# Banded scores on four quarters of the array, and five PSUM banks for the first batch's products, in a fused attention, channel-mix and gated-attention kernel

## The chip, the cores and the metric

One core of a Trainium2 chip runs the whole program. The metric is device time in microseconds (us), the median of the runs shown; lower is better. PE is TensorE, DVE VectorE, ACT ScalarE, POOL GpSimd; SP issues most of the DMAs. PSUM, where PE writes its products, has eight banks of 128 partitions x 512 fp32 numbers.

## The reference

Three stages follow each other, for 4 batches of 576 positions and 512 features (8 heads of 64).

```python
def _attn_ref(q, k, v):                      # stage 1: banded attention
    scores = scale * np.matmul(q, k.transpose(0, 1, 3, 2))
    mask_plain = (rel >= 0) & (rel < window)                                   # heads 0-3, window 32
    mask_dil = (rel >= 0) & (rel < window * dilation) & (rel % dilation == 0)  # heads 4-7, dilation 4
    scores = np.where(masks[None, :, :, :], scores, -1000000000.0)
    ...                                      # softmax over the keys
    return np.matmul(attn, v).astype(np.float32)

def _moe_ref(x, mu_k, mu_r, w_k, w_v, w_r):  # stage 2: channel mix
    xk = mu_k * x + (1.0 - mu_k) * x_prev
    xr = mu_r * x + (1.0 - mu_r) * x_prev
    k = np.maximum(xk @ w_k, 0.0)
    v = k * k @ w_v
    r = 1.0 / (1.0 + np.exp(-(xr @ w_r)))
    return (r * v).astype(np.float32)
# stage 3 (_moe2_ref): per position two of four experts, each a causal attention with its own
# wq, wk, wv, wo over the 576 positions
```

## The kernel before

**Stage 1.** A batch has four head pairs: pairs 0 and 1 with the plain window, 2 and 3 with the dilated one, whose positions are sorted by remainder first, so that both are a band. A pair's queries are cut into nine tiles of 64, each against 96 keys. `turn_qk` (L271, L276) makes qT and kT, in which one head of the pair has partitions 0 to 63 and the other 64 to 127. `attn_weights` computes the scores (`products`, L304): for each query tile one 64x64 weight load and 96 columns for each head; head 0 uses array rows 0 to 63 and writes output partitions 0 to 63, head 1 the other half of both. Query tiles 0 to 4 lie in one PSUM bank and 5 to 8 in a second, both with the tag `sc`. In fp32 a product is two passes, so a block of one pair is 2 x 9 x 2 = 36 PE rows. Then for each query tile DVE adds the mask, takes the minimum into `st` (L323) and leaves the scores in `pe`; ACT takes the exponential (L328), DVE scales by the reciprocal sum (L338 to L340). `attn_values`: PE transposes three query tiles of weights (`pt`, L368), ACT copies them (L369), PE multiplies by the values (`av`, L379), ACT copies the result into x (L394). For batches 2 and 3 the weights are turned by DVE and a round trip through DRAM instead, without `pt`. Batch 0's scores also accumulate a mask that PE adds from the identity.

For batch 1 the two banks' products are issued one after the other, each ahead of its own softmax part; for batches 2 and 3 both come first (L289 to L310).

**Stage 2.** Per batch and half c of 288 positions: 4 receptance products z (L532), 8 keys products h (L539), 4 value products v (L555). Each is 12 (z, h) or 24 (v) matmuls of 128x288, high and low parts of fp32 (`product`, L517 to L524). ACT reads z (tanh, L537) and h (ReLU, L543); DVE and ACT make the square's high part kh and low part kl from r (L547 to L553); x is overwritten with z times v (L559). The mixed inputs m, xh and xl come from x (L498 to L502 for batch 0, L513 and L514 for the others, where POOL makes xl).

**PSUM.** `ps` (L60) hands out banks by tag: sc 2, pt 2, av 1, mm 3. All products of stage 2 use `mm`. A tag's banks go round; a product waits until the bank's former content has been read.

**What sets the order.** `goal` (L714) and the loop after it set how many steps of attention (batches 1, then 2 and 3) are written between the steps of the channel mix (batches 0 to 3). A scheduler of the framework then orders each engine's instructions by its own estimates of time; within one engine they run in that order. `together_with(b, 2)` (L527) puts the score products of batches 2 and 3 behind the last matmul of `product` written so far. `load_qk` and `load_v` are issued by SP in order; the queries and keys of pair 2 of batch 1 come behind the mark "window". Names in the rows: sc_1_0_5 is the score bank of batch 1, pair 0, from query tile 5; h_0_1_6 the keys product of batch 0, half 1, slice 6; z_1_0_2 and v_0_1_0 likewise; pt_1_0_2 the third transpose of batch 1, pair 0. The number behind is a serial one.

Of the kernel before, what the change touches and what calls it, by code (L numbers as in the profile page):

```python
# [21 lines left out]
def tile_dilated_attention__rwkv_channel_mix__moe_attention(  # L22
# [17 lines left out]
    nc = tc.nc  # L40
# [5 lines left out]
    CH = 288  # L46
    QB = 64
    WK = QB + 32
# [11 lines left out]
    def ps(tag, name):  # L60
        return psum["pool"].tile([128, 512], F32, tag=tag, name=name, bufs=psum[tag])


    ident = cpool.tile([128, 128], F32, name="ident")
# [62 lines left out]
    def win(dil, t):  # L127

        if t == 0:
            return 0, m_first  # L130
        return QB * t - 32, (m_class.get(t, m_next) if dil else m_next)

    early = {}
# [91 lines left out]
    def attn_pair(ap, b, hp, loaded):  # L225

        qT, kT = turn_qk(ap, b, hp, loaded[0])
        yield
        pe = yield from attn_weights(ap, b, hp, qT, kT)
        yield from attn_values(ap, b, hp, loaded[1], pe)  # L230
# [50 lines left out]
    def attn_weights(ap, b, hp, qT, kT):  # L281

        dil = hp >= NP // 2
        nm = f"{b}_{hp}"
        pe = ap.tile([128, NT, WK], F32, tag="pe", name=f"pe_{nm}", bufs=2)
        st = ap.tile([128, 3, NT], F32, tag="st", name=f"st_{nm}", bufs=2)
        scs = {}

        def products(t0, t1):  # L289

            sc = scs[t0] = ps("sc", f"sc_{nm}_{t0}")
            n = t1 - t0
            if b == 0:
                for j in range(2):
                    h = slice(64 * j, 64 * j + 64)
                    nc.tensor.matmul(sc[h, : n * WK], early["ident"][h, h], early[int(dil)][h, t0:t1, :],
                                     start=True, stop=False)
            for t in range(t0, t1):
                k0, mask = win(dil, t)
                c0 = WK * (t - t0)  # L300
                with together_with(b, 2):
                    for j in range(2):
                        h = slice(64 * j, 64 * j + 64)
                        nc.tensor.matmul(sc[h, c0 : c0 + WK], qT[h, QB * t : QB * t + QB], kT[h, k0 : k0 + WK],  # L304
                                         start=(b > 0), stop=(b > 0 or t == t1 - 1))

        if b > 1:
            for t0, t1 in ((0, 5), (5, 9)):
                products(t0, t1)
            yield  # L310
        for t0, t1 in ((0, 5), (5, 9)):
            if b < 2:
                products(t0, t1)
            sc = scs[t0]
            n = t1 - t0
            if b == 0:
                nc.vector.tensor_reduce(out=st[:, 0, t0:t1], in_=sc[:, : n * WK].rearrange("p (t k) -> p t k", k=WK),
                                        axis=AX.X, op=ALU.min)
            for t in range(t0, t1):
                k0, mask = win(dil, t)  # L320
                c0 = WK * (t - t0)
                if b:
                    nc.vector.tensor_tensor_reduce(  # L323
                        out=pe[:, t, :], in0=sc[:, c0 : c0 + WK], in1=mask, scale=-0.125, scalar=BIG,
                        op0=ALU.add, op1=ALU.min, accum_out=st[:, 0, t : t + 1],
                    )
                if b or not t0 == 5:
                    nc.scalar.activation(  # L328
                        pe[:, t, :], pe[:, t, :] if b else sc[:, c0 : c0 + WK], AF.Exp, bias=st[:, 0, t : t + 1], scale=-1.0,
                        accum_out=st[:, 1, t : t + 1],  # L330
                    )
            if b == 0 and t0 == 5:
                pb = pe[:, t0:t1, :]
                nc.vector.tensor_tensor(pb, st[:, 0, t0:t1].unsqueeze(2).to_broadcast([128, n, WK]),
                                        sc[:, : n * WK].rearrange("p (t k) -> p t k", k=WK), op=ALU.subtract)
                nc.scalar.activation(pb, pb, AF.Exp)
                nc.vector.tensor_reduce(out=st[:, 1, t0:t1], in_=pb, axis=AX.X, op=ALU.add)
            nc.vector.tensor_scalar_add(st[:, 1, t0:t1], st[:, 1, t0:t1], 1e-9)  # L338
            nc.vector.reciprocal(st[:, 2, t0:t1], st[:, 1, t0:t1])
            marks["first weights"] = nc.vector.tensor_mul(pe[:, t0:t1, :], pe[:, t0:t1, :],  # L340
                           st[:, 2, t0:t1].unsqueeze(2).to_broadcast([128, n, WK])).ins
            yield
        return pe
# [14 lines left out]
    def attn_values(ap, b, hp, vw, pe=None, pT=None):  # L358

        dil = hp >= NP // 2  # L360
        nm = f"{b}_{hp}"
        av = None
        for i in range(3):
            if pT is None:
                pt = ps("pt", f"pt_{nm}_{i}")
                pts = ap.tile([WK, 384], F32, tag="pts", name=f"pts_{nm}_{i}", bufs=2)
                for a in range(3):
                    nc.tensor.transpose(pt[:WK, 128 * a : 128 * a + 128], pe[:, 3 * i + a, :], ident)  # L368
                nc.scalar.copy(pts, pt[:WK, :384])  # L369
            for a in range(3):  # L370
                t = 3 * i + a
                cuts = [(0, 64)] if t != 4 else [(0, 32), (32, 64)]
                for u0, u1 in cuts:
                    p0 = QB * t + u0
                    if p0 in (0, 288):
                        av = ps("pt" if pT is not None and p0 else "av", f"av_{nm}_{p0}")
                    with together_with(b, 2):
                        for j in range(2):
                            nc.tensor.matmul(  # L379
                                av[64 * j : 64 * j + 64, p0 % 288 : p0 % 288 + u1 - u0],  # L380
                                vw[:, j, t, :],
                                (pts[:, 128 * a + 64 * j + u0 : 128 * a + 64 * j + u1] if pT is None
                                 else pT[:, 2 * j + u0 // 32 : 2 * j + u1 // 32, t, :]),
                                start=True, stop=True,
                            )
                    p1 = QB * t + u1
                    if p1 in (288, 576):
                        hf = p1 // 288 - 1
                        if dil:
                            dst = X[b][:, hp, 1 : S + 1].rearrange("p (i r) -> p r i", r=4)  # L390
                            dst, src = dst[:, 2 * hf : 2 * hf + 2, :], av[:, :288].rearrange("p (r i) -> p r i", r=2)
                        else:
                            dst, src = X[b][:, hp, 1 + 288 * hf : 289 + 288 * hf], av[:, :288]
                        nc.scalar.copy(dst, src)  # L394
            if (hp, i) == (NP - 1, 2):
                complete.add(b)
            yield
# [129 lines left out]
    def together_with(b, first):  # L527


        return tc.issue_after(marks["product"]) if b >= first and "product" in marks else ExitStack()  # L530

    def receptance(dp, b, c, fo, z, xr, wts):  # L532
        p = ps("mm", f"z_{b}_{c}_{fo}")[:, :CH]
        product(p, wts["r"], xr, range(KT), slice(128 * fo, 128 * fo + 128))


        nc.scalar.activation(z[:, fo, :], p, AF.Tanh, scale=0.5)  # L537

    def keys(dp, b, c, fo, kh, kl, xk, wts):  # L539
        p = ps("mm", f"h_{b}_{c}_{fo}")[:, :CH]  # L540
        product(p, wts["k"], xk, range(KT), slice(128 * fo, 128 * fo + 128))
        r = dp.tile([128, CH], F32, tag="r", name=f"r_{b}_{c}_{fo}", bufs=2)
        nc.scalar.activation(r, p, AF.Relu)  # L543
        if b == 0 and 2 <= fo < 6:
            nc.scalar.activation(r, r, AF.Square)
            nc.scalar.activation(kh[:, fo, :], r, AF.Copy, scale=0.5)
            nc.vector.scalar_tensor_tensor(out=kl[:, fo, :], in0=r, scalar=0.5, in1=kh[:, fo, :].bitcast(F32),  # L547
                                           op0=ALU.mult, op1=ALU.subtract)
            return
        nc.vector.scalar_tensor_tensor(out=r, in0=r, scalar=0.5, in1=p if b else r, op0=ALU.mult, op1=ALU.mult)  # L550
        nc.scalar.copy(kh[:, fo, :], r)  # L551
        half = nc.gpsimd if b == 1 and fo % 2 == 0 and fo < FT - 2 else nc.vector
        half.tensor_sub(kl[:, fo, :], r, kh[:, fo, :].bitcast(F32))  # L553
# [82 lines left out]
    with tc.tile_pool(name="apool", bufs=2, side="left") as ap:  # L636
# [80 lines left out]
        stop = per + 6 * NP * 2 + 3  # L717
# [505 lines left out]
```

## Time and profile before

| | before |
|---|---|
| median of 3 runs | 554.2 us (553.92 to 554.38) |
| profiled execution, its own time | 553.32 us |
| its span in the trace | 551.5 us |
| PE busy | 534.1 us, 97% |
| DVE busy | 350.1 us, 63% |
| ACT busy | 337.9 us, 61% |
| POOL busy | 65.0 us, 12% |

The profile comes from one execution, 0.9 us faster than the median. Sums are made against its own time. Batch 1's attention lies from 88 to about 139 us, beside batch 0's keys and values; the attention of batches 2 and 3 follows, beside the channel mix of batches 1 and 2; stage 3 begins at 356 us. An engine's busy share is an average over these; what a change is worth has to be read in the stretch where it acts. In the timeline, neighbouring matmuls overlap by some 0.16 us (the pipeline), so that the distance of starts, not the duration, is a product's cost.

### The profile page before, as it was taken

The page shows a single profiled execution, that of the slowest core. Times are in us where ns is not written, and L with a number is a line of the kernel's source. Part 1 is how long each engine was busy: PE and PEld are TensorE (multiplying, and loading weights), DVE is VectorE, ACT ScalarE, POOL GpSimd, SP SyncE. Part 2 cuts the span into 40 slices and gives each one's busy share as a digit, 9 for nine tenths or more (in the row PEclk, how much of TensorE's full clock was granted, in tenths as well). Part 3 has the DMA queues.
Part 4 walks back from the last instruction along what each step waited for, and adds up shares of the span by engine and source line. Part 5 has one row for each costly group of instructions (what it writes and reads, how often), then busy time and mean ns, then how long its engine had stood idle before and what let it go on. Part 6 is the DMA issues. An engine that isn't in the chain of part 4 may idle for free.

```text
span 551.5 us, 12506 instructions
## 1 busy us (share of the span) xinstructions
PE 534.1 (97%) x4657; PEld 483.9 (88%) x4657; DVE 350.1 (63%) x1153; ACT 337.9 (61%) x959; POOL 65.0 (12%) x99
## 2 busy tenths in 40 slices
PE   8987989999999999999999999999999999999996
PEld 4657978989999999999999999999977988988763
DVE  3788989775766588276360526438686559566752
ACT  3789988575874484564453525237576667656862
POOL 8500000010342031221032203000000000000000
PEclk9997999999999999999999999999999999999999
DMA  9969386857545663130100420054605615324313
GB/s 168 240 184 285 91 214 144 151 108 137 103 113 128 141 140 79 42 97 13 54 1 1 92 63 1 1 130 97 163 5 126 177 31 130 93 75 115 112 39 96
DMA packets 130173, 57.66 MB, mean 105 GB/s; under 512 B 109928, under 2 KB 117184, under 8 KB 130112
## 3 DMA queue, kind: packets, MB, share of 16 engines
q1 hardware_dynamic: 129392, 55.88, 42.8%
q8 instruction: 37, 0.61, 0.5%
q0 software_dynamic: 416, 0.44, 0.4%
q10 hardware_dynamic: 304, 0.53, 0.3%
q14 instruction: 24, 0.20, 0.1%
HBM read 34.42 MB, written 10.03 MB: 81 GB/s over the span
## 4 chain that ended last, share of the span: by engine, by line
PE 85%; ACT 7%; DVE 5%; DMA 2%; issue 1%; SPq 0%; ACTq 0%; DVEq 0%
PE v L524 19%; PE h L524 14%; PE z L524 7%; PE av L1037 5%; PE pv L863 5%; PE po L1123 5%; PE sc L304 4%; PE pt L1000 4%; PE pq L524 4%; PE pk L524 4%; PE av L379 4%; PE sc L949 2%; PE sc L951 2%; PE idle L76 2%; PE pt L368 2%; DMA rqk<-in_q_dram 1%
## 5 line engine op out<-in xcount | busy, mean ns | idle before, releaser
L524 PE MATMUL h<-xh,wk_hi 128*128 128x288 f32 x256 | 76.7, 300 | 1.8 <-ACT r L543 1.7
L524 PE MATMUL h<-xl,wk_hi 128*128 128x288 f32 x256 | 75.7, 296 | 0.6 <-DVE xl L502 0.6
L524 PE MATMUL h<-xh,wk_lo 128*128 128x288 f32 x256 | 75.3, 294 | 0.0
L524 PE MATMUL v<-kh,wv_hi 128*128 128x288 f32 x256 | 74.9, 299 | 0.0
L524 PE MATMUL v<-kh,wv_lo 128*128 128x288 f32 x256 | 74.8, 297 | 0.0
L524 PE MATMUL v<-kl,wv_hi 128*128 128x288 f32 x256 | 74.5, 296 | 0.0
L961 ACT ACTIVATE pe<-pe,st 128x64 f32<-128x64 f32 (+4 forms) x80 | 44.8, 561 | 16.6 <-DVE st L955 16.1
L514 POOL TENSOR_TENSOR xl<-m,xh 128x576 fp32r<-128x576 f32 x24 | 34.7, 1461 | 152.4 <-ACT xh L513 152.4
L524 PEld LDWEIGHTS h<-xh,wk_hi 128*128 128x128 f32 x256 | 47.9, 187 | 3.3 <-ACT r L543 2.7
L524 PEld LDWEIGHTS h<-xl,wk_hi 128*128 128x128 f32 x256 | 48.1, 188 | 0.9 <-DVE xl L502 0.9
L524 PEld LDWEIGHTS v<-kh,wv_lo 128*128 128x128 f32 x256 | 47.8, 188 | 0.6
L524 PEld LDWEIGHTS v<-kh,wv_hi 128*128 128x128 f32 x256 | 47.6, 188 | 0.7 <-DVE r L550 0.2
L524 PEld LDWEIGHTS h<-xh,wk_lo 128*128 128x128 f32 x256 | 48.2, 188 | 0.0
L524 PEld LDWEIGHTS v<-kl,wv_hi 128*128 128x128 f32 x256 | 47.7, 188 | 0.2
L328 ACT ACTIVATE pe<-pe,st 128x96 f32<-128x96 f32 x108 | 39.0, 363 | 13.3 <-DVE st L323 13.3
L543 ACT ACTIVATE r<-h 128x288 f32<-128x288 f32 x64 | 25.6, 406 | 33.6 <-PE h L524 30.1
L955 DVE CUSTOM_DVE_ANT_0 pe<-sc,cmask 128x64 f32<-128x64 f32 (+4 forms) x80 | 33.1, 427 | 17.2 <-PE sc L951 16.7
L499 DVE SCALAR_TENSOR_TENSOR m<-x,mus,m 128x288 f32<-128x288 f32 x64 | 30.6, 517 | 16.3 <-ACT m L498 16.2
L553 DVE TENSOR_TENSOR kl<-r,kh 128x288 fp32r<-128x288 f32 x50 | 30.5, 615 | 15.6 <-ACT kh L551 15.5
L524 PE MATMUL z<-xh,wr_hi 128*128 128x288 f32 x128 | 39.3, 310 | 0.9 <-ACT z L537 0.9
L524 PE MATMUL z<-xl,wr_hi 128*128 128x288 f32 x128 | 38.4, 301 | 0.0
L524 PE MATMUL z<-xh,wr_lo 128*128 128x288 f32 x128 | 38.3, 300 | 0.0
(195 smaller groups left out, 1404.2 us busy)
## 6 DMA issues: line engine op xcount, KB each, us to landing
kk<-kh SPq DMA_DIRECT2D x32, 144.0 KB, 2.8
kl<-kl SPq DMA_DIRECT2D x32, 144.0 KB, 2.8
raw_in_moe_w_k_dram<-in_moe_w_k_dram SPq DMA_DIRECT2D x4, 1024.0 KB, 8.2
raw_in_moe_w_v_dram<-in_moe_w_v_dram SPq DMA_DIRECT2D x4, 1024.0 KB, 6.0
out_dram<-ob SPq DMA_DIRECT2D x14, 256.0 KB, 2.8
rqk<-in_q_dram SPq DMA_DIRECT2D x48, 72.0 KB, 2.5
rqk<-in_k_dram SPq DMA_DIRECT2D x48, 72.0 KB, 2.4
moved<-turned SPq DMA_DIRECT2D x8, 432.0 KB, 3.0
```

The costliest lines, as they stand in the source:

```text
L304: nc.tensor.matmul(sc[h, c0 : c0 + WK], qT[h, QB * t : QB * t + QB], kT[h, k0 : k0 + WK], start=(b > 0), stop=(b > 0 or t == t1 - 1))
L328: nc.scalar.activation(pe[:, t, :], pe[:, t, :] if b else sc[:, c0 : c0 + WK], AF.Exp, bias=st[:, 0, t : t + 1], scale=-1.0, accum_out=st[ ...
L499: nc.vector.scalar_tensor_tensor(out=m, in0=x, scalar=mus[:, 0, w, f : f + 1], in1=m, op0=ALU.mult, op1=ALU.add)
L514: nc.gpsimd.tensor_sub(lo[:, f], m[:, f], hi[:, f].bitcast(F32))
L524: marks["product"] = nc.tensor.matmul(o, w[:, kt, wsl], x[:, kt, :], start=(n == 0), stop=(n == last)).ins
L543: nc.scalar.activation(r, p, AF.Relu)
L553: half.tensor_sub(kl[:, fo, :], r, kh[:, fo, :].bitcast(F32))
L863: nc.tensor.matmul(p, x[:, kt, t0 : t0 + tn], w[:, kt, 512:772], start=(n == 0), stop=(n == 3 * KT - 1))
L955: nc.vector.tensor_tensor_reduce(out=pe[:tn, PO[t] + c0 : PO[t] + c1], in0=sc, in1=m, scale=-0.125, scalar=(BIG if i == 0 else st[:tn, 1, ...
L961: nc.scalar.activation(pb, pb, AF.Exp, bias=st[:tn, 0, t : t + 1], scale=-1.0, accum_out=st[:tn, 2, t : t + 1])
L1037: ins = nc.tensor.matmul(av1[p0 : p0 + 64, q0 - 64 : q1 - 64], vh[kb][:kn], w[:kn, c0 : c0 + q1 - q0], start=(kb == blocks[0]), stop=(kb = ...
L1123: nc.tensor.matmul(sums[t], x[:, t0 : t0 + 128], w[:, h, :], start=(h == 0 and n == 0), stop=(h == 1 and n == 2))
```

## The change

Two edits.

First, for batches 1 to 3 all 18 score products of a pair are issued together (`all_products`), in the order of query tiles 5, 0, 6, 1, 7, 2, 8, 3, 4. Query tiles 5 to 8 write the other half of the output partitions: head 0 in partitions 64 to 127, head 1 in 0 to 63. Rows 0 to 63 or 64 to 127 of the array with output half 0 or 1 make four 64x64 quarters. `attn_values` reads the heads of these query tiles from the swapped half. Batch 1 thus has both banks of scores before its first softmax; batch 0 is as before.

Second, `bank` gives batch 0's receptance and keys products banks by turns from mm, pt, mm, pt, mm: five banks for what had three. The 23rd of these products is h_0_1_6, and it gets `pt`.

```diff
@@ attn_weights
-            if b == 0:
-                for j in range(2):
-                    ...
+            for j in range(2):
+                h = slice(64 * j, 64 * j + 64)
+                nc.tensor.matmul(sc[h, : n * WK], early["ident"][h, h], early[int(dil)][h, t0:t1, :],
+                                 start=True, stop=False)
             for t in range(t0, t1):
                 k0, mask = win(dil, t)
                 c0 = WK * (t - t0)
-                with together_with(b, 2):
-                    for j in range(2):
-                        h = slice(64 * j, 64 * j + 64)
-                        nc.tensor.matmul(sc[h, c0 : c0 + WK], qT[h, QB * t : QB * t + QB], kT[h, k0 : k0 + WK],
-                                         start=(b > 0), stop=(b > 0 or t == t1 - 1))
+                for j in range(2):
+                    h = slice(64 * j, 64 * j + 64)
+                    nc.tensor.matmul(sc[h, c0 : c0 + WK], qT[h, QB * t : QB * t + QB], kT[h, k0 : k0 + WK],
+                                     start=False, stop=(t == t1 - 1))
+
+        def all_products():
+            for t0 in (0, 5):
+                scs[t0] = ps("sc", f"sc_{nm}_{t0}")
+            with together_with(b, 2):
+                for t in (5, 0, 6, 1, 7, 2, 8, 3, 4):
+                    k0 = win(dil, t)[0]
+                    c0 = WK * (t % 5)
                     for j in range(2):
                         h = slice(64 * j, 64 * j + 64)
+                        o = h if t < 5 else slice(64 - 64 * j, 128 - 64 * j)
+                        nc.tensor.matmul(scs[t // 5 * 5][o, c0 : c0 + WK], qT[h, QB * t : QB * t + QB], kT[h, k0 : k0 + WK],
+                                         start=True, stop=True)
+
+        if b >= 1:
+            all_products()
         if b > 1:
-            for t0, t1 in ((0, 5), (5, 9)):
-                products(t0, t1)
             yield
         for t0, t1 in ((0, 5), (5, 9)):
-            if b < 2:
+            if b < 1:
                 products(t0, t1)
@@ attn_values
+                            r = 1 - j if b and t > 4 else j
                             nc.tensor.matmul(
                                 av[64 * j : 64 * j + 64, p0 % 288 : p0 % 288 + u1 - u0],
                                 vw[:, j, t, :],
-                                (pts[:, 128 * a + 64 * j + u0 : 128 * a + 64 * j + u1] if pT is None
-                                 else pT[:, 2 * j + u0 // 32 : 2 * j + u1 // 32, t, :]),
+                                (pts[:, 128 * a + 64 * r + u0 : 128 * a + 64 * r + u1] if pT is None
+                                 else pT[:, 2 * r + u0 // 32 : 2 * r + u1 // 32, t, :]),
@@ receptance, keys
+    used = []
+
+    def bank(b):
+        if b:
+            return "mm"
+        used.append(b)
+        return ("mm", "pt", "mm", "pt", "mm")[len(used) % 5]
-        p = ps("mm", f"z_{b}_{c}_{fo}")[:, :CH]
+        p = ps(bank(b), f"z_{b}_{c}_{fo}")[:, :CH]
-        p = ps("mm", f"h_{b}_{c}_{fo}")[:, :CH]
+        p = ps(bank(b), f"h_{b}_{c}_{fo}")[:, :CH]
```

The code's lines move down: L304 before is L318 after, L524 is L539, L368 L382, L379 L394, L550 L575, L553 L578, L323 L337.

On PE, batch 2's pair 1 among batch 1's receptance products, before:

```order
L524 MATMUL z_1_0_1_2089<-xh_1_0_4_1873,wr_lo_252 128x288
L304 MATMUL sc_2_1_0_2105<-kT_2_1_2064,qT_2_1_2062 64x96 x10
L304 MATMUL sc_2_1_5_2116<-kT_2_1_2064,qT_2_1_2062 64x96 x8
L524 MATMUL z_1_0_2_2125<-xh_1_0_4_1873,wr_hi_251 128x288
L524 MATMUL z_1_0_2_2125<-xl_1_0_4_1874,wr_hi_251 128x288
```

And the end of the same block after the change:

```order
L318 MATMUL sc_2_1_5_2106<-kT_2_1_2064,qT_2_1_2062 64x96 x2
L318 MATMUL sc_2_1_0_2105<-kT_2_1_2064,qT_2_1_2062 64x96 x2
L318 MATMUL sc_2_1_5_2106<-kT_2_1_2064,qT_2_1_2062 64x96 x2
L318 MATMUL sc_2_1_0_2105<-kT_2_1_2064,qT_2_1_2062 64x96 x4
L539 MATMUL z_1_0_2_2125<-xl_1_0_4_1874,wr_hi_251 128x288
```

The two banks take turns by pairs of heads instead of coming one behind the other; the block stands one matmul further down among the same products.

On PE, batch 1's pair 0 and the keys product h_0_1_6, before:

```order
L524 MATMUL h_0_1_5_1362<-xh_0_1_3_995,wk_lo_272 128x288
L304 MATMUL sc_1_0_0_1287<-kT_1_0_1283,qT_1_0_1281 64x96 x10
L304 MATMUL sc_1_0_5_1329<-kT_1_0_1283,qT_1_0_1281 64x96 x8
L524 MATMUL h_0_1_6_1409<-xh_0_1_3_995,wk_hi_271 128x288
L524 MATMUL h_0_1_6_1409<-xl_0_1_3_996,wk_hi_271 128x288
```

After the change h_0_1_6 stands behind pair 0's transposes and first values:

```order
L394 MATMUL av_1_0_0_1355<-pts_1_0_0_1350,vw_1_1274 64x64 x6
L394 MATMUL av_1_0_0_1355<-pts_1_0_1_1381,vw_1_1274 64x64 x2
L394 MATMUL av_1_0_0_1355<-pts_1_0_1_1381,vw_1_1274 64x32 x2
L382 MATMUL pt_1_0_2_1396<-ident_66,pe_1_0_1285 96x128 x3
L539 MATMUL h_0_1_6_1409<-xh_0_1_3_995,wk_hi_271 128x288
L539 MATMUL h_0_1_6_1409<-xl_0_1_3_996,wk_hi_271 128x288
L539 MATMUL h_0_1_6_1409<-xh_0_1_3_995,wk_lo_272 128x288
```

Pair 0's scores now stand behind h_0_1_7 and, in front of its transposes, PE has 21 value products, pair 1's scores and 19 more value products. Of the values v_0_1_0, those that read slices 6 and 7 come after h_0_1_6.

On DVE, between pair 1's softmax and pair 2's of batch 1, before:

```order
L550 SCALAR_TENSOR_TENSOR r_0_1_7_1481<-r_0_1_7_1481 128x288
L339 RECIPROCAL st_1_1_1443<-st_1_1_1443 128x4
L340 TENSOR_TENSOR pe_1_1_1442<-pe_1_1_1442,st_1_1_1443 128x384
L553 TENSOR_TENSOR kl_0_1_1016<-r_0_1_6_1422,kh_0_1_1015 128x288
L553 TENSOR_TENSOR kl_0_1_1016<-r_0_1_7_1481,kh_0_1_1015 128x288
L271 STREAM_TRANSPOSE qT_1_2_1585<-rqk_1257 128x144x4
L271 STREAM_TRANSPOSE kT_1_2_1587<-rqk_1257 128x144x4
L271 STREAM_TRANSPOSE qT_1_3_1729<-rqk_1257 128x144x4
```

After:

```order
L271 STREAM_TRANSPOSE kT_1_2_1587<-rqk_1257 128x144x4
L271 STREAM_TRANSPOSE qT_1_3_1729<-rqk_1257 128x144x4
L584 SCALAR_TENSOR_TENSOR x0_212<-z_0_0_847,v_0_0_1_1703 128x288
L575 SCALAR_TENSOR_TENSOR r_0_1_6_1422<-r_0_1_6_1422 128x288
L575 SCALAR_TENSOR_TENSOR r_0_1_7_1490<-r_0_1_7_1490 128x288
L578 TENSOR_TENSOR kl_0_1_1016<-r_0_1_6_1422,kh_0_1_1015 128x288
L578 TENSOR_TENSOR kl_0_1_1016<-r_0_1_7_1490,kh_0_1_1015 128x288
L337 ISA pe_1_2_1589,st_1_2_1590<-sc_1_2_5_1592,m_next_104 128x96
```

The squares and low parts of slices 6 and 7 moved from before pair 2's turning of queries and keys to behind it, directly before pair 2's softmax, which begins with query tile 5 or later. On POOL the second low half xl of batch 1's first half now stands behind the clearing of the new rows of x.

## Rows read from the trace of the kernel before

**Rows 1.** The page: the span, and busy time of each engine.
```profile
span 551.5 us, 12506 instructions
PE 534.1 (97%) x4657; PEld 483.9 (88%) x4657; DVE 350.1 (63%) x1153; ACT 337.9 (61%) x959; POOL 65.0 (12%) x99
```

**Rows 2.** Stretches: bounds, length, busy per engine (count), granted clock, DMA share, GB/s.
```profile
45.72:49.97 4.25, 4.25 (x19) 4.25 (x18) 3.58 (x7) 3.26 (x7) 0.00 (x0) 0.50 1.13 316
62.00:88.14 26.14, 23.75 (x171) 22.41 (x169) 23.86 (x38) 22.01 (x45) 0.10 (x1) 1.00 0.79 206
88.14:139.41 51.27, 50.90 (x595) 46.50 (x595) 37.02 (x156) 33.96 (x131) 2.80 (x3) 1.00 0.68 126
139.41:356.00 216.59, 216.59 (x2012) 212.57 (x2012) 121.98 (x348) 115.03 (x336) 43.59 (x37) 1.00 0.28 66
```

**Rows 3.** PE's waits from 45 to 93: total us, times, longest.
```profile
PE h L524 <- ACT r L543: 1.7, 3, 1.2
PE z L524 <- ACT z L537: 0.9, 2, 0.6
PE h L524 <- DVE xl L502: 0.6, 1, 0.6
```

**Rows 4.** The chain of waits from 50 to 93: start, us, what.
```profile
69.26 1.10 DVE xl L502 x3
...
81.63 5.81 DMA rqk<-in_q_dram
```

**Rows 5.** The chain of waits from 155 to 172.
```profile
155.52 3.20 PE h L524 x24
158.72 1.63 PE sc L304 x36
...
163.75 1.31 PE av L379 x40
```

**Rows 6.** Timeline of PE, 98 to 99.3: start, us, what.
```profile
98.52 0.82 PE L368 MATMUL pt<-ident,pe 128*96 128x128 f32 x6
99.18 0.40 PE L524 MATMUL v<-kh,wv_hi 128*128 128x288 f32 x1
```

**Rows 7.** Instructions of L304 from 142 to 260: ns min/median/max, first and last.
```profile
L304 PE MATMUL sc<-kT,qT x252: 242/243/294, 142.5 to 255.4; 64*64 64x96 f32 x126
```

**Rows 8.** Timeline of PE, 88 to 139: scores and transposes of batches 1 and 2.
```profile
88.14 1.70 PE L304 MATMUL sc<-kT,qT 64*64 64x96 f32 x36
...
93.60 1.70 PE L304 MATMUL sc<-kT,qT 64*64 64x96 f32 x36 [0.37 <-DVE kT L276]
...
116.70 0.75 PE L368 MATMUL pt<-ident,pe 128*96 128x128 f32 x5
117.38 1.04 PE L304 MATMUL sc<-kT,qT 64*64 64x96 f32 x20
...
118.60 0.54 PE L304 MATMUL sc<-kT,qT 64*64 64x96 f32 x6
...
123.70 1.04 PE L304 MATMUL sc<-kT,qT 64*64 64x96 f32 x18
```

**Rows 9.** Timeline of DVE, 88 to 117: start, us, what, idle before and its releaser.
```profile
92.68 0.78 DVE L276 STREAM_TRANSPOSE kT<-rqk 128x576 f32<-128x576 f32 x1
...
96.29 0.46 DVE L553 TENSOR_TENSOR kl<-r,kh 128x288 fp32r<-128x288 f32 x1
...
97.02 0.66 DVE L340 TENSOR_TENSOR pe<-pe,st 128x480 f32<-128x480 f32 x1
...
105.99 1.19 DVE L271 STREAM_TRANSPOSE kT<-rqk 128x576 f32<-128x576 f32 x1 [0.69 <-DMA rqk<-in_k_dram]
...
111.66 0.26 DVE L323 CUSTOM_DVE_ANT_0 pe<-sc,m_next 128x96 f32<-128x96 f32 x1 [1.29 <-PE sc L304]
```

**Rows 10.** Timeline of POOL, 135 to 140.
```profile
138.02 1.43 POOL L514 TENSOR_TENSOR xl<-m,xh 128x576 fp32r<-128x576 f32 x1 [19.96 <-ACT xh L513]
139.38 0.19 POOL L124 MEMSET x<- 128x4 f32 x2
```

More of the change, by code (lines that the diff above doesn't have):

```diff
@@ L292, in products @@
             n = t1 - t0
-            if b == 0:
-                for j in range(2):
-                    h = slice(64 * j, 64 * j + 64)
-                    nc.tensor.matmul(sc[h, : n * WK], early["ident"][h, h], early[int(dil)][h, t0:t1, :],
-                                     start=True, stop=False)
+            for j in range(2):
+                h = slice(64 * j, 64 * j + 64)
+                nc.tensor.matmul(sc[h, : n * WK], early["ident"][h, h], early[int(dil)][h, t0:t1, :],
+                                 start=True, stop=False)
             for t in range(t0, t1):
```

## The prediction

> **What bounds the kernel now.** I read the page's first part, then the busy time in stretches. TensorE (PE) works 97% of the span, DVE, the next, 63% [rows 1]. The stretches show where this is strict: from 139.41 to 356 us, where the attention of batches 2 and 3 stands among the channel mix, PE is busy the whole time, 216.59 us; from 88.14 to 139.41 (batch 1's attention) 50.90 of 51.27; only from 62 to 88.14 does it lose 2.4 us [rows 2]. So a microsecond of PE taken out of the long stretch is a microsecond of time, and nothing else there is. The last stretch (from 356) isn't touched. PE's waits between 45 and 93 us name what the second part of the change works on: 1.7 us of keys products behind ACT's ReLU (three times) and 0.9 us of receptance products behind ACT's tanh, both because a product needs a PSUM bank that the reader has not given back, and 0.6 us behind DVE's low half xl [rows 3]. The chain of waits over the same time doesn't run through PE's banks but through that DVE subtraction and the loads of queries [rows 4]: there PE isn't the only bound.
>
> **Part 1: the scores on four array tiles.** A block (both heads, nine query tiles) is 18 products, each two passes: 36 rows. In the middle of the kernel it takes 1.63 us between keys products of 133 ns [rows 5]; the blocks of pair 0 and 1 of batch 1 read 1.70 with the last product's tail [rows 8]. The full array passes 128 columns of fp32 at about 110 ns: the six transposes' passes go from 98.52 to 99.18, 0.66/6 [rows 6]. For 96 columns that is 110 x 96/128 = 82 ns, an estimate. Two heads side by side then take 9 x 2 x 82 ns = 1.48 us, and with 0.15 of change-over 1.63, what the row says: the two tiles already run at once. With four, query tiles 0 to 4 (two of the array's quarters) and 5 to 8 (the two others) overlap; the fuller quarters hold 5 products: 5 x 2 x 82 = 0.82, plus 0.15 = 0.97. **A block saves 0.66 us.** No row shows four quarters at work. Bounds: nothing is saved, if quarters that share input rows take turns; or the rows come at the pace of the densest small products in the trace, the 40 rows of values in 1.31 us [rows 5], less 0.15, 29 ns each: 36 x 29 ns + 0.15 = 1.19, a saving of 0.44. I take 0.66: the two heads' rows start together now, so issue doesn't hold back a pair.
>
> The Trainium skill ("TensorEngine Tiling (Array Packing)", Tiling Modes) lists four independent 64x64 tiles; but its Gotcha 1: PSUM Pressure says that different row tiles cannot access the same PSUM bank simultaneously. By that the two heads of before, which write one bank, would take 36 x 82 ns + 0.15 = 3.1 us, an estimate; the trace's 1.63 disagrees [rows 5], so I don't let this rule count against the change, which keeps the two heads of one query tile in one bank.
>
> Blocks of batches 2 and 3: eight. Seven, 252 rows, lie after 142 us [rows 7], where PE is all [rows 2]. **Term A: 7 x 0.66 = 4.6 us** (0 to 4.6; 3.1 at the values' pace). On PE the order there hardly moves: the same products stand before and behind the block. DVE gets the upper tiles first, which it reads as fast; after 139 us each block has dozens of products between itself and its values.
>
> **Part 2, and batch 1, from 62 to 139.** Here the order changes, so I count PE's work and its new idle time. Batch 1's four blocks and batch 2's first (PE's scores at 123.70 [rows 8]) save 5 x 0.66 = 3.3. The wait for banks in the 62-88 stretch: five banks let the 1.7 us behind ACT's r go in part only, since ACT must still read each product, and ACT and DVE set the chain there [rows 4]; I take 1.0 (0 to 1.7). The tanh wait of 0.9 goes, but the first keys products then arrive that much earlier at the wait for xl: no gain.
>
> Against this stand three waits that the new order makes.
> - sc of pair 1. Pair 0's block now stands behind keys product h_0_1_7, and 21 value products stand between it and pair 1's block: PE gets there 0.97 + 21 x 0.133 = 3.8 us after pair 0's block began. DVE finished pair 1's kT 5.3 us after it before (92.68 + 0.78 - 88.14 [rows 8, 9]); pair 0's block starts about 0.6 later now (12 products of keys come ahead, 1.6, less the 1.0), and kT, which waits for its load, doesn't, so that it ends some 4.7 behind, less what DVE saves by no longer waiting for the second half: about 4.4. Idle 0.6.
> - pt of pair 0. PE reaches pair 0's transposes some 8.0 us after the block's start (3.8 + 0.6 + 0.97 + 19 x 0.133 = 7.9). They need pair 0's weights; the multiplication ended 97.68 - 88.14 = 9.5 after it before [rows 9], and now the lower tiles, which the first transposes need, come last on DVE, so about 10. Idle 2.0. Formerly PE stood at none of these.
> - z of batch 1. The last copy to x now has 26 products (8 value, 18 receptance) before features 2 and 3 are wanted; before it had 29 value products, and POOL finished the low half at 139.45 [rows 10], as z began. POOL now clears the new rows of x (0.19 us for two [rows 10]) before that low half, behind a value product's end. Idle 0.3.
> What is behind each in PE's queue is everything; nothing overtakes. Sum of idle: 2.9 less the 0.4 that sc of pair 1 waited before [rows 8]: 2.5. **Term B: 3.3 + 1.0 - 2.5 = 1.8, of which I take 1.5**, because keys product h_0_1_6 now shares a bank with pair 0's transposes and runs behind them: its kl and that of h_0_1_7 come on DVE directly ahead of pair 2's softmax (0.46 us for one kl [rows 9]), and the last six value products of the first slice wait for kl. A check by pair 2: its kT can't come before the loads, which SP issues in order; before it ended at 107.18 [rows 9], now about 106.8; DVE waited 1.29 us for the second half's scores then [rows 9], which goes and pays for the four operations; so pair 2's transposes stay near 116.4, 0.3 earlier than 116.70 [rows 8]. From there 22.7 us were left to 139.41, now less 1.2 (pair 3's 26 rows at 117.38 and 118.60 [rows 8] are already done) and 0.66: z at about 137.6. Bounds of B: +3.5 (banks give 1.7, idle 1.5) to -2.5 (no bank gain, idle 5.8).
>
> **Sum.** 4.6 + 1.5 = 6.1. The profiled execution took 553.3 us (span 551.5); its like with the change is 547.2. The median of the runs shown, 554.2, lies 0.9 above: **548.1**.
>
> **The rivals.**
> 1. Rows, not array time, set the pace: 29 ns a row in term A. A = 3.1, and B loses 5 x 0.22 = 1.1, so 0.4 + 0.9 = about 550.7 in all (553.3 - 3.5 + 0.9). For it: no product of this size in the trace goes quicker on the mean than 29 ns. Against: heads' rows start together now, and the values' 64 columns could be limited by the array itself (2 tiles x 55 ns / 2 = 27). The Trainium skill ("TensorE: Matmul & The Clock Gate", Wait — 56ns, not 53.3ns?) measures columns over 2.4 GHz plus 2.5 ns as the pace of back-to-back products, which no row of this change's size shows; taken as a floor a row it would lie near this case.
> 2. Quarters that share rows or columns take turns: A = 0, block still 1.63. B = 1.0 - 1.4 (PE arrives later, so waits less) = -0.4: 553.3 + 0.4 + 0.9 = 554.6. For it: no row shows four at once. Against: two at once are shown, and tiles in other halves.
> 3. Slower: batch 1's softmax becomes the bound from 88 to 139. Each of the four pairs' transposes now comes sooner after its scores (8.0 us for pair 0, 10.4 before); if PE stands 2.2 us at each, 8.8, and once its granted clock falls to half, as it did from 45.72 us (4.25 us at 0.50, that is 1.2 of 2.4 GHz, for 19 products [rows 2], 224 ns each against 133: 1.7 lost), then B = 3.3 + 1.0 - 8.8 - 1.7 = -6.2, and with A 4.6 the sum is -1.6: 555.8. It decides from 7 us of idle between 88 and 139 with one such fall, 8.9 without. For it: 0.37 us of idle there before leaves PE nothing to give; DVE is busy 37.0 of 51.3 [rows 2]. Against: loads, not DVE, hold pairs 2 and 3, and DVE's pauses for the second half go.
>
> **The numbers.** Forecast 0.54 (546.0 to 550.0), rival 1 0.22, rival 2 0.13, rival 3 0.11. About 0.2%, 1.1 us, is what a measurement can tell here. Faster: 0.53 + 0.21 + 0.02 + 0.01 = 0.77; within: 0.01 + 0.01 + 0.08 + 0.02 = 0.12; slower: 0.03 + 0.08 = 0.11. The range from 545.8 to 552.8 holds the first two cases and leaves out most of the last two.
>
> **What would show it.** A block's 36 rows in 0.97 us, without products between; 1.19 speaks for rival 1, 1.63 for rival 2. From batch 1's first receptance product to the end of the last value product 4.6 us less. PE's wait for ACT's tanh gone, that for r under 0.8; new waits of 0.6 for pair 1's kT and about 2 for pair 0's weights; z of batch 1 about 1.5 us earlier. I am wrong if PE idles over 5 us there, or if blocks keep their length.

## The result, and the profile after

| | before | after |
|---|---|---|
| median | 554.2 us (5 runs, 553.3 to 554.38) | 549.21 us (5 runs, 548.83 to 550.01) |
| ratio | | 0.9913, 95% interval 0.9902 to 0.9924 |
| span of the profiled execution | 551.5 us | 547.2 us |
| PE busy | 534.1 us | 525.8 us |

The change makes the kernel 5.0 us faster; 6.1 were forecast, 548.1 us. The page after begins (it answers to [rows 1]):

```profile
span 547.2 us, 12500 instructions
PE 525.8 (96%) x4653; PEld 476.1 (87%) x4657; DVE 350.8 (64%) x1153; ACT 336.4 (61%) x959; POOL 65.6 (12%) x99
```

PE has 8.3 us less to do and the span is only 4.3 us shorter: half of what was taken off PE came back as waiting. A block first. Timeline of PE after, one block and the next product (start, us, what); it answers to the block at 158.72 in [rows 5]:

```profile
156.38 1.05 PE L318 MATMUL sc<-kT,qT 64*64 64x96 f32 x36
157.36 0.40 PE L539 MATMUL h<-xh,wk_hi 128*128 128x288 f32 x1
```

From start to start 0.98 us, where it was 1.63. To compare the stretches I took them from the same place of the program, the first row of batch 2's pair 1, to the first product pv of stage 3 (6.4 us into that stage). Busy time there, first before, then after (columns as in [rows 2]):

```profile
142.53:362.45 219.92, 219.92 (x2038) 216.06 (x2037) 122.31 (x353) 114.01 (x335) 42.84 (x34) 1.00 0.26 63
```

```profile
141.85:358.13 216.28, 215.18 (x2031) 210.67 (x2031) 123.89 (x355) 114.12 (x338) 43.42 (x34) 1.00 0.27 64
```

After, seven 128x288 products more stand ahead of this block on PE (2031 rows are left, not 2038), and not one, as I read the order in the section on the change: 0.93 us at 133 ns. At equal work the part ahead of this place is therefore 142.53 - 141.85 + 0.93 = 1.6 us shorter, and the part behind it 219.92 - 216.28 - 0.93 = 2.7 us. The 2.7 is firm: three other runs with the same blocks and banks there (quarters alone, the last keys products in mm, the earlier split) give 2.7 to 2.8. The 1.6 is not: two later traces whose program is the same up to this place (a fourth bank, two of five) give 2.5 and 2.0. Before, PE never stood still there; after, it has two waits (waits of PE from 140 to 352: total, times, longest):

```profile
PE v L539 <- DVE r L575: 0.6, 1, 0.6
PE h L539 <- DVE r L575: 0.5, 1, 0.5
```

Waits of PE from 45 to 145 after, which answer to [rows 3] (the first line is left out; its 2.0 us belong to batch 0's attention, where the kernel before has the same wait):

```profile
...
PE v L539 <- ACT r L568: 1.9, 2, 1.2
PE sc L318 <- DVE kT L276: 0.9, 1, 0.9
PE h L539 <- ACT r L568: 0.8, 2, 0.5
PE sc L318 <- DVE kT L271: 0.7, 1, 0.7
PE pt L382 <- DVE pe L354: 0.7, 2, 0.5
...
```

The keys products' wait for ACT's ReLU fell from 1.7 to 0.8 and the tanh wait is gone, as forecast, but the value products right behind the blocks of pairs 0 and 1 now stand 1.9 us for ACT's ReLUs: PE got ahead, ACT didn't.

### The profile page after: what moved, and what is told of

It reads as the page before. It is cut to its first block, busy times and chain, and to the rows that moved or that the text cites. A ratio compares the mean times of both kernels' runs of the same rounds, so it can differ in the third digit from the quotient of the medians.

```text
span 547.2 us, 12500 instructions
## 1 busy us (share of the span) xinstructions
PE 525.8 (96%) x4653; PEld 476.1 (87%) x4657; DVE 350.8 (64%) x1153; ACT 336.4 (61%) x959; POOL 65.6 (12%) x99
## 4 chain that ended last, share of the span: by engine, by line
PE 73%; DVE 9%; ACT 7%; SPq 4%; DMA 3%; issue 2%; POOL 1%; DVEq 0%; ACTq 0%; POOLq 0%
PE v L539 16%; PE h L539 11%; PE z L539 5%; PE av L1062 5%; PE pv L888 5%; PE po L1148 5%; PE pt L1025 4%; PE pq L539 4%; PE pk L539 4%; PE av L394 2%; PE sc L974 2%; PE sc L976 2%; SPq L189 2%; PE idle L76 2%; ACT pe L342 1%
## 5 line engine op out<-in xcount | busy, mean ns | idle before, releaser
L539 PE MATMUL h<-xh,wk_hi 128*128 128x288 f32 x256 | 76.3, 300 | 1.3 <-ACT r L568 0.8
L539 PE MATMUL v<-kh,wv_hi 128*128 128x288 f32 x256 | 74.9, 299 | 2.5 <-ACT r L568 1.9
L539 PE MATMUL h<-xl,wk_hi 128*128 128x288 f32 x256 | 75.5, 295 | 0.3 <-DVE xl L517 0.3
L539 PE MATMUL h<-xh,wk_lo 128*128 128x288 f32 x256 | 75.3, 294 | 0.4 <-DVE wk_lo L688 0.4
L539 PE MATMUL v<-kh,wv_lo 128*128 128x288 f32 x256 | 74.7, 296 | 0.0
L539 PE MATMUL v<-kl,wv_hi 128*128 128x288 f32 x256 | 74.7, 297 | 0.0
L539 PEld LDWEIGHTS v<-kh,wv_hi 128*128 128x128 f32 x256 | 47.6, 188 | 3.5 <-ACT r L568 2.3
L539 PEld LDWEIGHTS h<-xh,wk_hi 128*128 128x128 f32 x256 | 47.8, 187 | 2.7 <-ACT r L568 1.3
L539 PEld LDWEIGHTS h<-xh,wk_lo 128*128 128x128 f32 x256 | 48.2, 188 | 0.7 <-DVE wk_lo L688 0.7
L539 PEld LDWEIGHTS h<-xl,wk_hi 128*128 128x128 f32 x256 | 48.1, 188 | 0.5 <-DVE xl L517 0.5
L539 PEld LDWEIGHTS v<-kh,wv_lo 128*128 128x128 f32 x256 | 47.8, 188 | 0.4
L539 PEld LDWEIGHTS v<-kl,wv_hi 128*128 128x128 f32 x256 | 47.7, 188 | 0.4
L578 DVE TENSOR_TENSOR kl<-r,kh 128x288 fp32r<-128x288 f32 x50 | 31.1, 627 | 16.5 <-ACT kh L576 16.2
L539 PE MATMUL z<-xl,wr_hi 128*128 128x288 f32 x128 | 38.8, 304 | 0.1
L539 PE MATMUL z<-xh,wr_hi 128*128 128x288 f32 x128 | 38.8, 308 | 0.0
L539 PE MATMUL z<-xh,wr_lo 128*128 128x288 f32 x128 | 37.9, 299 | 0.0
```

The lines of the kernel that those rows point to most:

```text
L539: marks["product"] = nc.tensor.matmul(o, w[:, kt, wsl], x[:, kt, :], start=(n == 0), stop=(n == last)).ins
```

## The experiments

All ratios are to the kernel before, with 95% intervals. My first theory: the five banks cost what batch 1's stretch lost; rival: issuing both halves of batch 1's scores early costs it.

**Four quarters alone.** `bank` returns "mm" always.

```diff
-        if b:
+        if True:
             return "mm"
```

> The scores on four quarters as in the changed kernel, all products of the channel mix in three mm banks as before. Theory (the banks are what batch 1's stretch lost to: PE runs ahead in batch 0's keys, then stands at value products 1.2 and 0.75 us for ACT's ReLU, and h_0_1_6 goes behind pair 0's transposes): blocks of 0.99 us, the stretch after batch 1 about 4.7 us shorter as in the changed kernel, batch 1's first z product about 2 us earlier than before, no wait of a value product for ACT; 547.2 us. Rival (issuing both halves of batch 1's scores ahead of its softmax, with the upper tiles first, is what costs; the banks cost nothing): z no earlier than before, waits at pair 0's transposes remain, 549.0 to 549.6 us.

Measured 549.16 us, 0.9913 (0.9900 to 0.9926): the same as the whole change. The theory fell: without the five banks PE stands for ACT's ReLU all the same, now before keys products (3.0 us in four waits, the longest 1.3, in the waits from 45 to 145).

**Five banks alone.** The kernel before with `bank` for z and h of batch 0.

> The five banks for batch 0's receptance and keys products alone, scores as before on two quarters. Theory: PE's idle before batch 1 falls from 2.4 to about 1.7 us but comes back as waits of value products for ACT's ReLU (1 to 2 us) and at pair 0's transposes, partly behind blocks of 1.63; 554.2 to 555.5 us. Rival (the banks help and the scores' order costs): about 1 us gained, 552.8 to 553.5 us.

553.57 us, 0.9994 (0.9985 to 1.0003): no change that can be told. The first theory's wait of value products is there (1.0 us); its loss isn't.

**Two quarters, all else changed.**

```diff
-                        o = h if t < 5 else slice(64 - 64 * j, 128 - 64 * j)
+                        o = h
-                            r = 1 - j if b and t > 4 else j
+                            r = j
```

> Both parts of the change, with its issue order (5, 0, 6, 1, ...) and two banks, but query tiles 5 to 8 write the same output half as tiles 0 to 4, so that only two quarters of the array are used. Theory (the gain is the four quarters running at once): blocks back at 1.63 us, seven of them cost 4.5 us again, about 1 us of idle in batch 1 is filled; 554.0 to 556.0 us. Rival (the order by itself, or alternate banks, lets products overlap): blocks of about 1.0 us and 549.2 us.

553.01 us, 0.9986 (0.9977 to 0.9995), and in its timeline a block is back at 1.63:

```profile
158.07 1.70 PE L318 MATMUL sc<-kT,qT 64*64 64x96 f32 x36
159.70 0.40 PE L539 MATMUL h<-xh,wk_lo 128*128 128x288 f32 x1
```

So the gain is the quarters' running at once, 549.21 against 553.01, 3.8 us; order and banks together are worth about 0.9.

**Quarters in turn.** The query tiles issued as 0 to 8.

```diff
-                for t in (5, 0, 6, 1, 7, 2, 8, 3, 4):
+                for t in range(NT):
```

> The changed kernel with the same four quarters, but the query tiles issued in the order 0 to 8, so that first only two quarters are fed (tiles 0 to 4) and then the other two (5 to 8). Theory (PE takes its queue in order; quarters overlap only where neighbours in the queue use different ones): blocks of 1.55 to 1.63 us, 553.0 us as with two quarters. Rival (each quarter takes its products as soon as it is free): blocks of about 1.0 us, 549.2 us.

551.49 us, 0.9958 (0.9942 to 0.9973), between the two. The block takes 1.36:

```profile
158.69 1.44 PE L318 MATMUL sc<-kT,qT 64*64 64x96 f32 x36
160.05 0.40 PE L539 MATMUL h<-xh,wk_hi 128*128 128x288 f32 x1
```

Both expectations missed: placing alone gives 0.27 of the 0.65, the alternating order the rest. The block is shortened where the queue passes from one pair of quarters to the other: judged by the starts in the trace, the second pair's first pass comes 0.56 us into the block, while each quarter of the first pair has three passes to go (at 0.63, 0.71 and 0.79).

**The last keys products of batch 0 in mm.**

```diff
-        return ("mm", "pt", "mm", "pt", "mm")[len(used) % 5]
+        return "mm" if len(used) > 20 else ("mm", "pt", "mm", "pt", "mm")[len(used) % 5]
```

> The changed kernel, but from the 21st product of batch 0's receptance and keys on (h_0_1_5 on) the banks are mm alone, so that h_0_1_6 stands where it was before. Theory: the value products' wait for ACT's ReLU becomes smaller since 24 keys products stand between pair 0's and pair 1's scores again, the wait for pair 1's kT stays; 548.0 us (1.2 better than the changed kernel). Rival (the scores' early issue costs): 549.2 us, no change.

549.05 us, 0.9912 (0.9899 to 0.9926): no change. That h_0_1_6 stands behind pair 0's transposes costs nothing. My theory on the banks was done with, and I formed two others. In batch 1's stretch the chain over loads, weight splits and softmax sets the time, whatever PE saves; behind it PE waits for banks that DVE has not read.

**Quarters for batches 2 and 3 only.** `if b >= 2: all_products()`, batch 1's products and all banks as before.

> Four quarters for batches 2 and 3 only; batch 1's scores as before (two quarters, one half ahead of its own softmax), three mm banks as before. Theory (batch 1's stretch is set by the chain of loads, weight splits and softmax on SP, DVE and ACT, so that its four shorter blocks buy nothing): eight blocks of 0.99 us, no new idle before batch 1's z, 549.0 to 549.8 us, as the changed kernel. Rival (each block is worth its 0.65 us wherever it stands): 2.6 us worse than the changed kernel, 551.8 us.

548.55 us, 0.9908 (0.9894 to 0.9922): as fast as the whole change. Batch 1's four blocks on four quarters bought little, and the medians show only a sum. From batch 2's pair 1 to stage 3 this run takes 216.41 us, where quarters alone (the run that differs in batch 1's scores only) takes 216.24 + 0.93 at equal work, 0.8 more, since PE stands for r twice there and once here. The medians differ by 0.6 (549.16 less 548.55), so ahead of that place batch 1's blocks gave back some 0.2 us (0.8 in the two traces, from the first receptance product on) of the 2.6 that four blocks take off PE.

What holds that stretch can be followed in the trace after. DVE's last split of w_v frees the space for batch 1's values. It ends at 95.79; pair 1's kT had ended at 93.88:

```profile
93.10 0.78 DVE L276 STREAM_TRANSPOSE kT<-rqk 128x576 f32<-128x576 f32 x1
...
94.57 1.22 DVE L688 TENSOR_TENSOR wv_lo<-raw_in_moe_w_v_dram,wv_hi 128x1024 fp32r<-128x1024 f32 x1
```

SP issues the values' loads right behind, and only behind them pair 2's queries and keys:

```profile
93.90 1.93 SPq L176 DMA_DIRECT2D rqk<-in_k_dram  x4
95.94 0.44 SPq L204 DMA_DIRECT2D vw<-in_v_dram  x1
...
101.96 3.21 SPq L176 DMA_DIRECT2D rqk<-in_k_dram  x4
```

I took the split for what releases the values' loads. The rows don't bear that out: SP was busy until 95.83 with the keys of pair 3, which go where pair 1's were and so wait for pair 1's kT. In all fourteen traces these loads start 0.03 us after pair 1's kT ends, and the values' first load is issued 0.10 us behind them, when the split has been over for 0.14 to 0.59 us. DVE then waits for pair 2's keys (timeline of DVE; the brackets are the idle time and what ended it), and PE 0.7 us for DVE:

```profile
107.28 1.16 DVE L271 STREAM_TRANSPOSE kT<-rqk 128x576 f32<-128x576 f32 x1 [0.61 <-DMA rqk<-in_k_dram]
```

From the end of pair 1's kT to the end of pair 2's it is 13.7 to 14.6 us in all fourteen traces: 107.18 - 93.45 = 13.73 before, 108.44 - 93.88 = 14.56 after. That is the steady distance of a chain.

**The split written one step earlier.** `"v3": 42` becomes `"v3": 41`.

> The changed kernel with the split of the last quarter of w_v written one step earlier, so that DVE's part of it stands ahead of pair 0's softmax instead of in the middle of it. Theory (this split holds the space into which batch 1's values are loaded, and behind that load SP holds pair 2's queries and keys, so that the split's end sets when pair 2's kT comes): kT of pair 2 comes 0.3 to 0.8 us earlier and its scores wait less than 0.70 us; 548.7 us. Rival (the load of the split's own data or the slots of the queries set it): no change, 549.2 us.

549.92 us, 0.9935 (0.9921 to 0.9949): not faster, perhaps slower. The split ended at 95.36, in a trace that began 0.4 us sooner, so no earlier. Pair 1's kT ended at 93.88 and SP issued the values' first load at 95.94, both as in the trace after, though the split was over 0.43 us sooner: what holds this chain is pair 1's slot, the expectation's rival, and not DVE's place for the split.

What the move cost shows in the same trace. ACT reached its part of the split earlier and stood longer for its data (2.29 us instead of 1.39), with the ReLUs queued behind it, and PE's value products for those (2.4 us in two waits, the longest 2.2; after, 1.9 and 1.2). Behind the wait of 2.2 us, at a time when PE had been busy for 1.51 of 3.70 us, the granted clock fell (from 91.1 to 94.5 us; columns as in [rows 2]):

```profile
91.10:94.50 3.40, 3.40 (x16) 3.40 (x15) 3.40 (x23) 3.40 (x13) 0.00 (x0) 0.50 0.46 77
```

At 0.50, 1.2 of 2.4 GHz, the value products start 240 ns apart instead of 133; for the 14 that do, it is 1.5 us. How much of the 0.7 us between the medians is the wait and how much the clock isn't shown. Moving an instruction forward in a queue that waits for data moved the wait, and everything behind it paid.

**A fourth bank for later keys.** Every fourth keys product of batches 1 to 3 takes a pt bank.

```diff
+    def bank_of_keys(b):
+        if b == 0:
+            return bank(b)
+        later.append(b)
+        return ("mm", "mm", "mm", "pt")[len(later) % 4]
-        p = ps(bank(b), f"h_{b}_{c}_{fo}")[:, :CH]
+        p = ps(bank_of_keys(b), f"h_{b}_{c}_{fo}")[:, :CH]
```

> The changed kernel, and every fourth keys product of batches 1 to 3 takes a pt bank instead of an mm bank. Theory (the two new waits of PE for DVE's r after batch 1, 0.54 and 0.57 us, are for mm banks that DVE has not yet read): both go and the stretch from batch 2's second block to stage 3 is about 1 us shorter, 548.2 us. Rival (DVE and ACT are late themselves, and PE waits for their output sooner or later): the waits move to the value products, 549.2 us.

546.66 us, 0.9871 (0.9856 to 0.9886): 2.5 us better than the change. Its trace shows no wait of PE from 140 to 350, and the same stretch is

```profile
140.95:355.26 214.31, 214.31 (x2030) 210.51 (x2030) 123.31 (x355) 114.51 (x338) 43.63 (x34) 1.00 0.27 65
```

At equal work that is 219.92 - 214.31 - 0.93 = 4.7 us under before. What the bank had been held for shows on DVE in the trace after, ahead of the wait at 167.84: its queue of softmax work, mixing and the turning of weights stands before r, which reads the product's bank.

```profile
164.37 1.30 DVE L354 TENSOR_TENSOR pe<-pe,st 128x480 f32<-128x480 f32 x1
165.59 0.51 DVE L514 SCALAR_TENSOR_TENSOR m<-x,mus,m 128x288 f32<-128x288 f32 x1
166.02 1.06 DVE L363 STREAM_TRANSPOSE turned<-pe 128x864 f32<-128x864 f32 x1
...
167.35 0.43 DVE L575 SCALAR_TENSOR_TENSOR r<-r,h 128x288 f32<-128x288 f32 x1
```

```profile
167.84 0.40 PE L539 MATMUL h<-xh,wk_hi 128*128 128x288 f32 x1 [0.54 <-DVE r L575]
```

The second wait, at 203.66, follows four such mixing operations in one row (201.26 to 203.25) in the same way.

**The fourth bank without the rest.** The kernel before with that rule (batch 0 in mm).

> The kernel before, and nothing but every fourth keys product of batches 1 to 3 in a pt bank. Theory (before, PE never stood for a bank in that stretch, so a fourth bank is only worth something with the shorter blocks): 553.7 us, no change. Rival (the bank by itself is worth 2.5 us): 551.2 us.

552.93 us, 0.9985 (0.9976 to 0.9994). The expectation was no change; 1.0 us is small, but its interval lies below 1. In the stretch after batch 1, where PE waits for nothing in either, it takes 219.82 us against 219.92: the bank is worth 0.1 there without the short blocks, 2.0 with them. Its trace is 0.6 us shorter in all, and that lies in stage 3 (from pv on 188.2 us against 189.1), which no edit touches and which takes 188.1 to 189.4 in the fourteen traces. So the 1.0 isn't shown to be the bank's.

**The same bank with fewer of the change's parts.** Quarters for batches 2 and 3 only:

> Four quarters for batches 2 and 3 only (batch 1 and batch 0's banks as before), and every fourth keys product of batches 1 to 3 in a pt bank. Theory (batch 1's blocks and batch 0's banks buy nothing; the four quarters and the fourth bank after batch 1 buy all): as e8, 546.0 to 546.7 us. Rival (batch 1's blocks begin to count once the later waits are gone): 548 us.

547.84 us, 0.9892 (0.9879 to 0.9906). And quarters for all three batches, batch 0 in mm:

> Four quarters for batches 1 to 3, batch 0's products in three mm banks as before, every fourth keys product of batches 1 to 3 in a pt bank. Theory (the five banks of batch 0 buy nothing): 546.7 us, as e8. Rival (they count once the later waits are gone): 548 us.

547.41 us, 0.9883 (0.9868 to 0.9898). Both lie 0.8 to 1.2 us above the version with everything, the first nearer to its rival's 548 than to the theory, with intervals that overlap its own: whether batch 0's five banks and batch 1's quarters begin to count here is open. What isn't: from batch 2's pair 1 to stage 3 both reach the 4.7 us at equal work.

**Two of five keys products in pt.** `("mm", "pt", "mm", "pt", "mm")[len(later) % 5]`.

> The changed kernel, and the keys products of batches 1 to 3 take mm and pt banks by turns as batch 0's do, two of five in pt. Theory (one more bank already ends the waits): 546.7 us, as e8. Rival (pt banks, which the second half of each pair's values shares, are held too long and the values wait): 548 us or more.

545.76 us, 0.9853 (0.9839 to 0.9866), the fastest of all, 3.5 us under the change. The stretch is 214.30 us, as with one in four; what it has beyond that run isn't there. In the two profiles it lies in stage 3 (543.9 - 355.75 = 188.15 us against 544.6 - 355.26 = 189.34), which no edit touches, and the intervals overlap: a true difference between the two isn't shown.

## Why the prediction was right, and where it was not

Between the two profiled executions, for which the sum was made, the saving is 553.3 - 548.9 = 4.4 us. That the medians miss the 6.1 by less, with 5.0, is chance: the profiled execution before lay 0.9 us under its median, the one after 0.3.

**A block.** Forecast 0.97 us by 82 ns a pass and five products in the fuller quarters; measured 0.98. The trace bears the mechanism out: the first passes of the four quarters start 6 to 7 ns apart, and the passes of one quarter, from its second on, some 82 ns apart. Rival 1 is out: 36 rows in 0.98 us are 27 ns each with the change-over, and (0.98 - 0.15)/36 = 23 without, under the values' 29. Rival 2, blocks of 1.63, is out by the 0.98 itself, and the two-quarters run shows that the quarters do it and not the order.

The pace that the prediction sets beside rival 1 from the Trainium skill ("TensorE: Matmul & The Clock Gate", Wait — 56ns, not 53.3ns?), columns over 2.4 GHz plus 2.5 ns, would be 42.5 ns for a row of 96 columns, an estimate, and 1.5 us for 36 rows. That is not near rival 1, as the prediction says, and as a floor a row the trace's 27 ns disagrees with it.

**Term A, 4.6 forecast, 2.7 measured.** This is the term that was mis-sized, by 1.9 us, and it is the step of the prediction that failed. Its blocks saved what was said, 7 x 0.65 = 4.5. What failed is "a microsecond of PE taken out of the long stretch is a microsecond of time": the view showed that PE waited for nothing before, not how close behind the others were. With shorter blocks DVE's reading of the keys' banks came late twice. Idle time on the page, 1.1 us, understates it: a product starts 133 ns after the last but is drawn 0.29 long, so a wait of 0.54 lengthens the distance of starts by 0.70 (167.01 to 167.84, less 0.13). The two cost 1.4; some 0.4 more lies in shorter delays. The bank for the keys gave the full 4.7 back, which shows the mechanism and its price.

**Term B, 1.5 forecast, 1.6 measured, on parts that were not.** All three waits named came: at pair 1's kT (0.9, forecast 0.6), at pair 0's transposes (0.5, forecast 2.0) and at batch 1's z (0.3 as forecast, in delays too short for the page's waits: 31 products from 137.30 to 141.85 at 133 ns leave 0.4 us over, the 24 before 0.1). The first came on other parts than were added: kT ended 6.1 us after pair 0's block began, not 4.4, and PE got there 5.1 after it, not 3.8, for the value products had stood for ACT's ReLU. These 1.9 were not foreseen, nor the 0.7 for pair 2's kT. That kT I put 0.4 earlier than before, and it came 1.3 later (108.44 against 107.18); but with the kernel before and a fourth bank, where nothing up to there is changed, it came at 108.48, so that the 1.3 isn't shown to be the change's.

Counted by distances of starts, three terms missed. The five blocks saved 3.8 us, not 3.3 (9.5 in all before, 5.7 after without their waits): before, three of them stood in three pieces each and took 2.1 us each instead of 1.63. From the first receptance product to pair 0's block, 264 products took 42.42 us and 276 take 41.84 after; over 133 ns each that leaves 7.3 and 5.1, so 2.2 less, where I took 1.0 for the banks. From there to batch 2's pair 1 the waits grew by 4.1, where I said 2.5. Together that is 3.8 + 2.2 - 4.1 = 1.9, less 0.25 by which the first receptance product began later (45.97, not 45.72). That the sum agrees is largely luck: misses of 0.5 and 1.2 stand against one of 1.6. And the runs say that its parts don't add up as I wrote them: the banks alone give 0.4, which can't be told from nothing, and batch 1's blocks little.

**Rival 3** was the right mechanism in the wrong size: PE idles 4.3 us from 88 to 139, not 7 to 9, and the granted clock stayed at 1.00 from 62 us to stage 3. In the run with the earlier split it did fall there, behind a wait of 2.2 us.

## What to carry to other kernels

Work taken off an engine that never waits was worth its full length only as far as the engines behind it had slack: read how late the buffers it writes are freed, and shorten that with the work. A stretch in which a chain of loads and slots sets the pace gave little back, however busy PE looked; a distance that stays the same across variants points to such a chain, and what releases each link must be read at that link: here the split ended just ahead of the load, and a queue of loads held it. Small products gained most from quarters of the array when neighbours in the queue used all four.

## What the runs showed of the hardware

Four 64x64 quarters run at once with two heads of one query tile in the same PSUM bank in different halves of the partitions: 36 passes of 96 columns in 0.98 us against 1.63 with two quarters, and 1.36 with four in an order that feeds two first. Quarters that share output partitions of one bank weren't tried.
